# q and k padded from 40 to 48 rows per half in an mLSTM mixer kernel

## The chip, the cores and the metric

One Trainium2 chip, one core. The metric is the device time of one execution in microseconds (us), measured without the profiler; the profile is one more execution, taken by the hardware profiler.

## What is computed

Two layers over 4 batches of 768 tokens. The first is a gated linear attention (mLSTM) with 8 heads of 40 channels, the second a token mixer and a channel MLP.

```python
# per batch and head, for t in range(768):   (q, k, v: 40 channels)
C = f_stab * C + i_stab * outer(v[t], k[t])
n = f_stab * n + i_stab * k[t]
y[t] = sigmoid(o[t]) * (C @ q[t]) / max(abs(n @ q[t]), 1)
# x: the heads side by side, 768 x 320 per batch
u = x + (relu(x.T @ w_tok1) @ w_tok2).T
out = u + relu(u @ w_ch1) @ w_ch2
```

## The kernel before

The recurrence is done in chunks of 128 tokens: 6 chunks for each of 4 batches, 24 units (b, c). Inside a unit the scores of all 8 heads are a 128 x 128 matrix each: k times q over 40 channels (`st_s`, line 308, 16 instructions in PE's trace per 8 heads), which VectorE multiplies by a decay matrix (`st_p`, line 318); the product meets v on TensorE (`st_pv`, line 436). What comes from earlier chunks is a state C (`st_state`: line 374 reads it, line 382 updates it). The token mixer (`a_part`, `halves_b`) and the channel MLP (`gemm1`, `gemm1w`, `gemm2`) follow.

Batch 0 goes first, before there is anything else for TensorE to do; its six units run in the loop of lines 973 to 1032, each after the other, and the weights are decoded meanwhile: they come as 8-byte words by DMA (`dec_load`, line 650, tile `wst`) and pass ScalarE (lines 661 and 665), VectorE (line 679), ScalarE again (line 691) and GpSimd (line 697). From about 58 us on, the MLP of one batch and the attention of the next are interleaved on TensorE.

For the scores, q and k of a unit lie in HBM as `qk[b, c, hf]`: two halves of four heads, each 40 rows (channels) of 4,096 bytes (q and k, 4 heads, 128 tokens, f32). `load_qk` (line 220) brings half `hf` into partitions 64*hf to 64*hf+39 of the tile `raw`, of which there are three, used in turn by units 0, 1, 2, 3 and so on. The unused partitions 40 to 63 and 104 to 127 are never read: the matmul of line 308 takes `64 * hf:64 * hf + D`, D = 40.

Nearly every transfer is issued from SyncE's queue in the order of the program. In the start-up that order is: gates f (the gates i and the identity come from ScalarE's queue), qk of units 0 and 1 (four transfers), kv of unit 0, two `sig` (output gate), q3 of unit 1, qk of unit 2, kv of unit 1, q3, kv of unit 2, two `wst`, qk of units 3 and 4 (four transfers), two more `wst`, and so on. The loads of unit 3 stand at lines 948 and 949, those of unit 4 at 982 and 983. The scores take the two halves in turn, so they need both from their second head on:

```python
305        for h in range(4):
306            for hf in range(2):
307                r = t["raw"][64 * hf:64 * hf + D]
308                nc.tensor.matmul(t["s"][hf][:, h, :], r[:, 1, h, :], r[:, 0, h, :], start=True, stop=True)
```

ScalarE's order in the loop matters below too: for a unit c it first decodes two weight pieces (lines 661 and 665, twice), then makes `xh` (line 487), then `pq` (line 269) and `wcol` (line 145) of the unit after, which free a bank of the PSUM pool `ps_h` (two banks) for the next `spread_split` (lines 168, 183, 186).

Of the kernel before, what the change touches and what calls it, by code (L numbers as in the profile page):

```python
# [17 lines left out]
B, H, S, D = 4, 8, 768, 40  # L18
L = 128
NC = S // L  # L20
E1 = D + 1
DM = H * D
DT, DF = 256, 1536
NF = DF // 128
G3 = 3 * E1
HP = 9
# [9 lines left out]
def kernel(ctx: ExitStack, tc: tile.TileContext, gates, qk, q3, kv, og,  # L36
                            wt1, wt2, wc1, wc2, ident, out):
    nc = tc.nc
# [14 lines left out]
    def load_sig(b, i):  # L53
        t = ap.tile([128, NC // 2, DM], F32, tag="sig", name="sig", bufs=3)
        nc.sync.dma_start(out=t, in_=og[b].rearrange("(c p) e -> p c e", p=128)[:, 3 * i:3 * i + 3, :])
        sig[(b, i)] = t
# [47 lines left out]
    def state_mask():  # L104
        nc.gpsimd.memset(bm_t, 1.0)
        bm4 = bm_t.rearrange("p (g i e) -> p g i e", g=3, i=3)
        for s in (1, -1):
            nc.gpsimd.affine_select(bm4, bm4, pattern=[[0, 3], [-s * D, 3], [0, E1]], compare_op=ALU.is_ge,
                                    fill=0.0, base=0 if s > 0 else D - 1, channel_multiplier=s)
# [38 lines left out]
    def rows_w():  # L148
        w_row = sp.tile([128, DM + H * E1], F32, tag="kv", name="w_row")
        xpool[3] = w_row = w_row[0:B * HP, 0:(NC - 1) * L].rearrange("p (c t) -> p c t", t=L)  # L150
        p = phi.rearrange("p (c t) -> p c t", t=L)[:, 0:NC - 1, L - 1:L]
        nc.gpsimd.tensor_tensor(w_row, b_t[:, 0:(NC - 1) * L].rearrange("p (c t) -> p c t", t=L),
                                p.to_broadcast([B * HP, NC - 1, L]), ALU.add)
# [66 lines left out]
    def load_qk(u, hf):  # L220
        b, c = u
        t = T.setdefault(u, {})
        if hf == 0:
            t["raw"] = raws[units.index(u) % 3]
        nc.sync.dma_start(out=t["raw"][64 * hf:64 * hf + D], in_=qk[b, c, hf])

    def load_phi(u):
        b, c = u
# [7 lines left out]
    def load_kv(u):  # L236
        b, c = u
        if b == 0 and c == 2:
            kvt = sp.tile([128, DM + H * E1], F32, tag="kv", name="kvt")
        else:  # L240
            kvt = ap.tile([128, DM + H * E1], F32, tag="kv", name="kvt")
        nc.sync.dma_start(out=kvt, in_=kv[b, c * L:(c + 1) * L, :])
# [48 lines left out]
    def prep_kw(u):  # L291
        b, c = u
        if c == NC - 1:
            return
        t = T[u]
        kw = ap.tile([128, H * E1], F32, tag="kw", name="kw", bufs=2)
        kw = kw[:, 0:DM].rearrange("p (h d) -> p h d", d=D)
        nc.gpsimd.tensor_tensor(kw, t["kv"][:, 0:DM].rearrange("p (h d) -> p h d", d=D),
                                wcol[:, c, HP * b:HP * b + H].unsqueeze(2).to_broadcast([128, H, D]), ALU.mult)
# [228 lines left out]
    def att(b):  # L528
        for c in range(NC):
# [17 lines left out]
            if n2 and not ahead:  # L547
                load_qk(n2, 0)
                if joined(n1):
                    load_qk(n2, 1)  # L550
# [22 lines left out]
            if n2 and not ahead:  # L573
                if not joined(n1):
                    load_qk(n2, 1)
                if not th:
                    load_q3(n2)
# [345 lines left out]
    t = ps_m.tile([128, HP], F32, tag="m", name="gw")  # L923
# [254 lines left out]
def _layout(q, k, v, i_gate, f_gate, o_gate, moe_w_tok1, moe_w_tok2, moe_w_ch1, moe_w_ch2):  # L1178
    import numpy as np

    c = np.ascontiguousarray
    qt, kt = q.transpose(0, 1, 3, 2), k.transpose(0, 1, 3, 2)
    qk = np.stack([qt, kt], 1)[:, :, np.argsort(ROW)]
    qk = c(qk.reshape(B, 2, 2, 4, D, NC, L).transpose(0, 5, 2, 4, 1, 3, 6))
    q3 = np.zeros((B, 9, D, S), np.float32)
    q3[:, :H] = qt
    q3 = c(q3.reshape(B, 3, 120, NC, L).transpose(0, 3, 2, 1, 4))
    v1 = np.concatenate([v, np.ones((B, H, S, 1), np.float32)], 3)
    kv = c(np.concatenate([k.transpose(0, 2, 1, 3).reshape(B, S, DM),
                           v1.transpose(0, 2, 1, 3).reshape(B, S, H * E1)], 2))  # L1190
    og = c(o_gate.transpose(0, 2, 1, 3).reshape(B, S, DM))
    gates = np.zeros((2, B, HP, S), np.float32)
    gates[:, :, ROW] = np.stack([i_gate, f_gate])
    gates = gates.reshape(2, B * HP, S)

    bits = lambda a: c(a).view(np.int64)
    wt1 = bits(moe_w_tok1.reshape(NC, 128, DT).transpose(1, 0, 2).reshape(128, NC * DT))
    wt2 = bits(moe_w_tok2.reshape(2, 128, S).transpose(1, 0, 2).reshape(128, 2 * S))
    r3 = list(range(320)) + list(range(256, 320))
    wc1 = bits(moe_w_ch1[r3].reshape(3, 128, NF, 128).transpose(1, 2, 0, 3).reshape(128, NF * 384))  # L1200
    wc2 = bits(moe_w_ch2.reshape(NF, 128, DM).transpose(1, 0, 2).reshape(128, NF * DM))
    return dict(gates=gates, qk=qk, q3=q3, kv=kv, og=og, wt1=wt1, wt2=wt2, wc1=wc1, wc2=wc2,
                ident=np.eye(128, dtype=np.float32))
# [21 lines left out]
```

## Time and profile before

| | |
|---|---|
| Time, three executions without the profiler | 424.15, 423.2, 423.2 us (median 423.2) |
| The profiled execution's own time | 426.41 us |
| Its span, first to last instruction | 424.7 us |
| TensorE matmul busy | 98% of the span |
| VectorE, ScalarE, GpSimd busy | 65%, 43%, 33% |
| Mean granted TensorE clock | 0.996 of full |
| DMA | 52.34 MB |

The page gives the busy share of each engine in 40 slices of the span, with the granted TensorE clock and the DMA engines' share below; the chain of work that ended last; who waited for whom; and for a chosen stretch the sum of each engine's work. DMA share is the mean busy share of the core's 16 DMA engines, so 0.62 is ten of them.

### The profile page before, as it was taken

How to read it: one execution, taken by the hardware profiler on the slowest of the kernel's cores; microseconds unless marked ns; L12 is line 12 of the kernel's file. 1: busy time of each engine (PE TensorE's matmuls, PEld its weight loads, DVE VectorE, ACT ScalarE, POOL GpSimd, SP SyncE). 2: the span in 40 equal slices, each digit the busy share in tenths (PEclk: the TensorE clock that was granted, in tenths of full speed). 3: DMA queues.
4: the chain of work that ended last, by engine and by line, in shares of the span. 5: the costliest groups of instructions: out<-in, count | busy, mean ns of one | idle time of the engine just before them, and what ended most of it. 6: DMA issues, size and time to landing. Idle time of an engine off the chain costs nothing.

```text
span 424.7 us, 8974 instructions
## 1 busy us (share of the span) xinstructions
PE 417.6 (98%) x3504; PEld 396.4 (93%) x3504; DVE 277.9 (65%) x620; ACT 183.1 (43%) x429; POOL 139.7 (33%) x185
## 2 busy tenths in 40 slices
PE   8989999999999999999999999999999999999996
PEld 4879998889999999999999999999999999988996
DVE  7967665424867598799796698789786647111412
ACT  2768568794535546343334346234144112111111
POOL 7367678752544320340350230331441110000000
PEclk9989999999999999999999999999999999999999
DMA  7997758960785722443355031432420000000000
GB/s 204 261 271 235 252 180 292 293 177 15 242 238 186 213 69 78 150 117 102 111 162 184 31 109 31 145 119 89 125 86 32 0 22 12 0 0 2 33 30 31
DMA packets 24574, 52.34 MB, mean 123 GB/s; under 512 B 2565, under 2 KB 13325, under 8 KB 24533
## 3 DMA queue, kind: packets, MB, share of 16 engines
q1 hardware_dynamic: 24293, 51.61, 39.6%
q8 instruction: 27, 0.44, 0.4%
q10 hardware_dynamic: 240, 0.18, 0.1%
q14 instruction: 14, 0.11, 0.1%
HBM read 47.73 MB, written 4.04 MB: 122 GB/s over the span
## 4 chain that ended last, share of the span: by engine, by line
PE 95%; DMA 3%; DVE 1%; issue 0%; DVEq 0%
PE acc L703 30%; PE ps_h L824 21%; PE ps_h L850 11%; PE ps_sc L308 6%; PE ps_b L703 5%; PE ps_a L703 5%; PE po L436 5%; PE pu L382 3%; PE po L405 3%; DMA raw<-in_qk_dram 2%; PE po L374 2%; PE po L412 2%; PE ps_t L771 1%; PE ps_t L769 1%; PE ps_t L770 1%; DMA i_t<-in_gates_dram 1%
## 5 line engine op out<-in xcount | busy, mean ns | idle before, releaser
L824 PE MATMUL ps_h<-uT,c1h 128*128 128x256 f32 x480 | 91.4, 282 | 0.0
L703 PE MATMUL acc<-c2h,gh 128*128 128x320 f32 x288 | 89.0, 318 | 0.0
L836 ACT ACTIVATE gh<-ps_h 128x512 fp32r<-128x512 f32 x48 | 28.7, 598 | 135.5 <-PE ps_h L824 111.1
L703 PE MATMUL acc<-c2l,gh 128*128 128x320 f32 x288 | 86.4, 309 | 0.0
L824 PEld LDWEIGHTS ps_h<-uT,c1h 128*128 128x128 f32 x480 | 75.9, 188 | 0.5
L824 PE MATMUL ps_h<-uT,c1l 128*128 128x256 f32 x256 | 66.1, 281 | 0.0
L703 PE MATMUL acc<-c2h,gl 128*128 128x320 f32 x288 | 61.8, 309 | 0.0
L837 DVE SCALAR_TENSOR_TENSOR gl<-ps_h,gh 128x512 fp32r<-128x512 f32 x48 | 33.0, 687 | 40.0 <-ACT gh L836 39.5
L703 PEld LDWEIGHTS acc<-c2h,gh 128*128 128x128 f32 x288 | 54.1, 188 | 1.4
L703 PEld LDWEIGHTS acc<-c2l,gh 128*128 128x128 f32 x288 | 54.1, 188 | 0.9
L854 DVE SCALAR_TENSOR_TENSOR gl<-ps_h,gh 128x512 fp32r<-128x512 f32 x24 | 16.6, 691 | 49.1 <-ACT gh L853 49.1
L824 PEld LDWEIGHTS ps_h<-uT,c1l 128*128 128x128 f32 x256 | 48.1, 188 | 0.0
L703 PEld LDWEIGHTS acc<-c2h,gl 128*128 128x128 f32 x288 | 47.2, 188 | 0.0
L455 POOL TENSOR_TENSOR sig<-sig,ht 128x320 f32<-128x320 f32 x18 | 14.8, 822 | 97.7 <-DVE ht L416 89.8
L289 ACT ACTIVATE dd<-dd,bcol 128x128 f32<-128x128 f32 x144 | 45.8, 392 | 1.4 <-POOL dd L279 1.3
L850 PE MATMUL ps_h<-uT,c1h 128*128 128x512 f32 x120 | 36.0, 394 | 0.0
L318 DVE TENSOR_TENSOR dd<-ps_sc,dd 128x512 f32<-128x512 f32 x48 | 30.9, 682 | 6.9 <-PE ps_sc L308 6.8
L507 POOL TENSOR_TENSOR xl<-x,xh 128x320 fp32r<-128x320 f32 x18 | 15.8, 880 | 51.4 <-DVE xh L505 50.0
L853 ACT ACTIVATE gh<-ps_h 128x512 fp32r<-128x512 f32 x24 | 14.3, 595 | 41.2 <-PE ps_h L850 41.2
L308 PE MATMUL ps_sc<-raw 40*128 40x128 f32 x384 | 27.5, 281 | 1.9 <-DMA raw<-in_qk_dram 1.7
L308 PEld LDWEIGHTS ps_sc<-raw 40*128 40x128 f32 x384 | 23.7, 187 | 5.0 <-issue 2.1
L850 PEld LDWEIGHTS ps_h<-uT,c1h 128*128 128x128 f32 x120 | 22.1, 188 | 3.9
(151 smaller groups left out, 857.0 us busy)
## 6 DMA issues: line engine op xcount, KB each, us to landing
dd<-phi_d SPq DMA_DIRECT2D x18, 512.0 KB
wst<-in_wc_dram SPq DMA_DIRECT2D x22, 384.0 KB
kvt<-in_kv_dram SPq DMA_DIRECT2D x24, 324.0 KB
raw<-in_qk_dram SPq DMA_DIRECT2D x48, 160.0 KB
sig<-in_og_dram SPq DMA_DIRECT2D x8, 480.0 KB
out_dram<-x SPq DMA_DIRECT2D x24, 160.0 KB
q3t<-in_q_dram SPq DMA_DIRECT2D x20, 180.0 KB
wst<-in_wt_dram SPq DMA_DIRECT2D x8, 384.0 KB
```

Of the source, the lines that this page charges most:

```text
L289: nc.scalar.activation(dd[:, h, :], dd[:, h, :], AF.Exp, bias=bcol[:, c, HP * b + h:HP * b + h + 1])
L308: nc.tensor.matmul(t["s"][hf][:, h, :], r[:, 1, h, :], r[:, 0, h, :], start=True, stop=True)
L318: nc.vector.tensor_tensor(dd, t["s"][hf], dd, ALU.mult)
L436: nc.tensor.matmul(o, t["dd"][:, ROW[h], :], x, start=c == 0 and h == 0, stop=h == H - 1)
L455: nc.gpsimd.tensor_tensor(sg, sg, ht[:, :, 0:D], ALU.mult)
L507: nc.gpsimd.tensor_tensor(xl, x, f32(xh), ALU.subtract)
L703: nc.tensor.matmul(ps, a, m, start=(first and i == 0), stop=(last and i == n - 1))
L824: nc.tensor.matmul(ps[:, j, :], c1[x][:, a:a + 128], u[:, y, :], start=not opened and part is first and i == 0 and (order == 0 and not clo ...
L836: nc.scalar.activation(gh, ps, AF.Relu)
L837: nc.vector.scalar_tensor_tensor(gl, ps, 0.0, f32(gh), op0=ALU.max, op1=ALU.subtract)
L850: nc.tensor.matmul(ps, c1[x][:, a:a + 128], u[:, :, y, :], start=n == 0, stop=n == len(todo) - 1)
L854: nc.vector.scalar_tensor_tensor(gl, ps, 0.0, f32(gh), op0=ALU.max, op1=ALU.subtract)
```

## The change

The host lays q and k out with 48 rows per half, of which the last 8 are zeros, and `load_qk` brings all 48. Each transfer grows from 163,840 to 196,608 bytes. The matmuls read the same 40 rows as before; the number and the order of instructions on every engine are the same.

```diff
@@ -19,6 +19,7 @@
 E1 = D + 1
+DP = 48
 DM = H * D
@@ -222,7 +223,7 @@
         if hf == 0:
             t["raw"] = raws[units.index(u) % 3]
-        nc.sync.dma_start(out=t["raw"][64 * hf:64 * hf + D], in_=qk[b, c, hf])
+        nc.sync.dma_start(out=t["raw"][64 * hf:64 * hf + DP], in_=qk[b, c, hf])
@@ -1181,7 +1182,8 @@
     qk = np.stack([qt, kt], 1)[:, :, np.argsort(ROW)]
-    qk = c(qk.reshape(B, 2, 2, 4, D, NC, L).transpose(0, 5, 2, 4, 1, 3, 6))
+    qk = qk.reshape(B, 2, 2, 4, D, NC, L).transpose(0, 5, 2, 4, 1, 3, 6)
+    qk = c(np.concatenate([qk, np.zeros_like(qk[:, :, :, :DP - D])], 3))
```

## Rows read from the trace of the kernel before

**Rows 1.** The page, its head and sections 1 and 2.

```profile
span 424.7 us, 8974 instructions
PE 417.6 (98%) x3504; PEld 396.4 (93%) x3504; DVE 277.9 (65%) x620; ACT 183.1 (43%) x429; POOL 139.7 (33%) x185
...
PEclk9989999999999999999999999999999999999999
```

**Rows 2.** Who waited, TensorE alone, whole span: total us, times, longest.

```profile
PE ps_sc L308 <- DMA raw<-in_qk_dram: 1.7, 2, 1.0
PE warm L897 <- POOL zero L61: 1.4, 1, 1.4
PE ps_phi L183 <- DVE z L178: 0.4, 1, 0.4
```

**Rows 3.** Timeline of TensorE, 14 to 38 us: start, us, work, [idle before].

```profile
15.72 1.74 PE L308 MATMUL ps_sc<-raw 40*128 40x128 f32 x16
...
21.93 0.38 PE L186 MATMUL ps_phi<-id,z 128*128 128x512 bf16 x1
23.29 0.46 PE L308 MATMUL ps_sc<-raw 40*128 40x128 f32 x2 [0.98 <-DMA raw<-in_qk_dram]
24.44 1.13 PE L308 MATMUL ps_sc<-raw 40*128 40x128 f32 x14 [0.69 <-DMA raw<-in_qk_dram]
...
31.22 0.38 PE L168 MATMUL ps_phi<-late_b,id_b 128*128 128x512 bf16 x1
...
31.97 1.16 PE L308 MATMUL ps_sc<-raw 40*128 40x128 f32 x16
```

**Rows 4.** The chain of work that ended last, 0 to 60 us: start, us, what.

```profile
15.05 9.25 DMA raw<-in_qk_dram
...
25.91 1.35 PE po L374 x6
27.26 1.16 PE pu L382 x6
28.41 2.31 PE po L436 x16
...
33.48 0.79 PE po L374 x6
34.27 0.60 PE pu L382 x6
34.87 1.79 PE po L436 x16
```

**Rows 5.** Windows: length, busy by engine (PE, PEld, DVE, ACT, POOL), PEclk, DMA share, GB/s.

```profile
0.00:24.30 24.30, 20.84 (x172) 14.77 (x172) 19.93 (x41) 13.77 (x24) 14.54 (x32) 1.00 0.87 234
3.00:4.00 1.00, 1.00 (x4) 0.38 (x3) 0.69 (x2) 0.48 (x1) 0.91 (x2) 1.00 0.62 180
20.00:25.00 5.00, 3.33 (x33) 2.50 (x34) 3.16 (x12) 3.87 (x8) 4.58 (x7) 1.00 1.01 245
25.96:29.37 3.41, 3.41 (x18) 3.41 (x18) 1.47 (x4) 1.99 (x4) 0.73 (x1) 0.50 0.94 299
44.00:48.00 4.00, 4.00 (x34) 4.00 (x33) 2.63 (x10) 2.75 (x7) 3.83 (x6) 1.00 1.02 386
```

**Rows 6.** Timeline of SyncE's queue: DMA issues in the order of the program.

```profile
1.64 1.91 SPq L225 DMA_DIRECT2D raw<-in_qk_dram  x4
...
7.70 0.80 SPq L225 DMA_DIRECT2D raw<-in_qk_dram  x2
...
14.02 3.64 SPq L225 DMA_DIRECT2D raw<-in_qk_dram  x4
18.04 1.25 SPq L650 DMA_DIRECT2D wst<-in_wt_dram  x2
```

**Rows 7.** Timeline of ScalarE, 19 to 36 us.

```profile
28.46 0.52 ACT L661 ACTIVATE pf<-wst 128x384 f32<-128x384 f32 x1 [0.38 <-DMA wst<-in_wt_dram]
...
30.18 0.17 ACT L145 ACTIVATE wcol<-ps_q 128x9 f32<-128x9 f32 x1
```

**Rows 8.** Timeline of GpSimd, 16 to 25 us.

```profile
23.74 0.74 POOL L298 TENSOR_TENSOR kw<-kvt,wcol 128x320 f32<-128x320 f32 x1
```

## Prediction

> **What bounds the kernel now.** The page first: TensorE's matmuls are busy for 417.6 of 424.7 us [rows 1]. So a change to transfers can only pay where TensorE waits for one, or runs slowly because it waited. The list of its waits is short [rows 2]: 1.4 us at the very start, 0.4 us for VectorE, and 1.7 us in two waits for the transfer of q and k into `raw`. No wait of TensorE for any other transfer is in it, and none for `raw` after the start-up. The other 36 transfers of q and k, for batches 1 to 3, therefore cost nothing now.
>
> The timeline shows the two waits [rows 3]. The last matmul before ends at 22.31 (21.93 + 0.38). The scores of unit 3 begin at 23.29 after 0.98 us, do two matmuls and wait 0.69 us more for the other half, whose transfer was issued at 15.05 and took 9.25 us, to 24.30 [rows 4]. A third, smaller one hides in a busy row: the 16 score matmuls of unit 2, at 15.72, take 1.74 us, where the same 16 take 1.16 at 31.97 [rows 3], so 0.58 us are lost. Together 0.58 + 0.98 + 0.69 = 2.25 us.
>
> Then the clock. [...] What it costs is read from the chain, where the same work stands at both levels [rows 4]: 1.35 against 0.79, 1.16 against 0.60, 2.31 against 1.79 us, so 0.56 + 0.56 + 0.52 = 1.64 us. All that this change can give in the profiled execution is therefore 2.25 + 1.64 = 3.9 us.
>
> Why is the transfer late? From 20 to 25 us the 16 DMA engines are busy all the time (share 1.01) at 245 GB/s [rows 5]. The transfers are not short of issue, they stand in line: 9.25 us from issue to landing for 160 KB.
>
> **The change part by part.** *The engines.* From 3 to 4 us, when q and k of units 0 and 1 are nearly all that moves, the share is 0.62: ten of sixteen engines [rows 5]. 40 rows over ten engines are 4 packets of 4,096 bytes for each. I take it that 48 rows go over sixteen, 3 packets each. [...]
>
> *Price of a packet.* In the crowded window an engine moves 245 / (16 x 1.01) = 15.2 GB/s, so 4,096 bytes take 0.27 us; in the best window, 44 to 48 us, 386 / (16 x 1.02) = 23.7 GB/s and 0.17 us [rows 5]. Up to the transfer that lands at 24.30, eight of these transfers are issued: 4, 2, and the first 2 of the 4 from 14.02 on [rows 6]. The engines that carry them lose 8 packets each: 8 x 0.17 to 8 x 0.27 = **1.4 to 2.2 us earlier**, middle 1.8. The six others get 24 packets more, but they had none of these; all sixteen now carry the same.
>
> *Check by bytes, for a limit that all engines share.* By 24.3 us 234 GB/s x 24.3 us = 5.69 MB have moved [rows 5]. What stands in line up to that transfer, with the 8 padded ones, is 4.99 MB (gates 0.22, identity 0.07, q and k 1.57, three kv 1.00, two `sig` 0.98, two q3 0.37, two `wst` 0.79). The rest, 0.7 MB, are later transfers that the free engines have taken ahead. Even if the total rate stays 245 GB/s, the padded transfer lands 0.7 / 0.245 = 2.8 us earlier, because nothing runs ahead of it. Both ways of counting give a gain; I take 1.8, with 1.4 and 2.8 as ends.
>
> *At unit 2* six transfers are ahead: 6 x 0.17 = 1.0 us at least, more than the 0.58 us lost. That goes. *At unit 3* TensorE is then ready at 22.31 - 0.58 = 21.73, and the half lands at 24.30 - 1.8 = 22.5, so some 0.8 us of waiting stay and TensorE gains 1.8 us there. *The clock:* 0.8 us of idling instead of 1.67. The 0.58 us lost at 15.7 and the 0.4 us at 7.0 [rows 2, 3] were followed by no dip, so I take it that the slow stretch goes too: 1.8 + 1.64 = 3.4 us.
>
> *What is late next.* GpSimd's `kw` ends at 24.48 [rows 8]; TensorE would want it at 27.26 - 1.8 - 0.56 = 24.9 [rows 4]: just covered. ScalarE is tighter. The second L168 matmul, now at 31.22 [rows 3], needs the bank that L145 frees at 30.35, and that work stands behind two weight decodes, the later of which waits for its transfer until 28.46 [rows 7]. That transfer is the second `wst` after 18.04, with ten of the padded ones ahead of it [rows 6]: 10/8 x 1.8 = 2.25 us earlier (1.7 to 2.7 by packets). The bank is then free at 28.1, so TensorE cannot be more than 31.22 - 28.1 = 3.1 us ahead there (2.6 to 3.6). This is the smaller of 3.4 and 3.1: **the sum is 3.1 us.**
>
> *What costs nothing.* 1.57 MB more over 48 transfers: after 60 us the queue has slack and TensorE no wait for it [rows 2]. Instructions, their order and the matmuls are unchanged.
>
> The profiled execution took 426.41 us, so the sum makes it 423.3; the median of the runs without the profiler is 3.2 us lower, 423.2, and I take the same 3.1 us off it: **420.1 us**, 419.3 (all 3.9) to 420.6 (2.6) for this case.
>
> **The rivals.** *The slow clock stays.* 0.8 us of idling may still be followed by it; then TensorE gains only the 1.4 to 2.2 us of the landing: 421.4. For it: the row shows one dip and cannot tell which length of idling starts one.
>
> *The waits are the profiler's.* Profiled, the kernel takes 3.2 us longer than without, and waits plus slow clock come to 3.9 us. If recording slows the transfers, the plain runs may already have the half of unit 3 in time; then at most 0.7 us can be had: 423.0, no change. Against it: the transfers stand in line at a share of 1.0 over some 20 us, and such a line doesn't vanish by a small speed-up; the 3.2 us can also be a slower issue everywhere.
>
> *The rows' place is the limit, not the engines.* All 48 rows of a half go to partitions of one half of the tile, as the 40 did. If what bounds such a transfer is where it writes, sixteen engines share what ten had, and 20% more bytes take 20% longer. From 3 to 4 us these transfers ran at 180 GB/s [rows 5]: 163,840 bytes are 0.91 us, 196,608 are 1.09, so 0.18 us more each. The sixth makes unit 2 wait 1.1 us longer, the eighth lands 8 x 0.18 = 1.5 us later, at 25.8 instead of 24.30, and TensorE with it: 424.7, and more if the slow clock lasts longer. It decides as soon as that half lands after 24.30. [...]
>
> **How the numbers follow.** A measurement of this kernel can tell about 0.3%, 1.3 us, from no change. Forecast 0.50 and the clock that stays 0.13 are faster (0.02 more for gains in between): 0.65. The profiler's waits, 0.20, are no change. The ports, 0.15, are slower. The likeliest is 420.1. The range reaches from all 3.9 us gained (419.3, a little under for the byte count) over 421.4 and 423.0 to 423.9, and leaves out mainly the ports: 419.1 to 423.9.
>
> **What would show it.** Right: a DMA share near 1.0 from 3 to 5 us instead of 0.62; the half of unit 3 landing between 21.5 and 22.9; the 16 matmuls of unit 2 in about 1.16 us; no PEclk below full before the end; L145 of unit 3 ending near 28.1 with TensorE behind it by little. Wrong: a share of 0.62 or below (still ten engines), the half landing at 24.3 or later (the ports), or the waits gone from the profile and the time the same (the profiler).

## Result: slower by 1.2%

| | before | changed |
|---|---|---|
| median of 6 runs | 423.54 us | 428.64 us |
| lowest to highest | 423.2 to 424.15 | 426.44 to 431.72 |
| ratio, 95% interval | | 1.0121 (1.0079 to 1.0163) |
| profiled execution | 426.41 us, span 424.7 | 426.44 us, span 424.7 |

Ratios, here and below, are formed without runs that took over 1.5% more than the fastest of their kernel.

The two profiled executions took the same time, and that is a trap: the profiled one of before was slower than all six plain runs of that kernel, and the profiled one of the changed kernel was its fastest. So the two pages agree while the medians are 5.1 us apart. More profiles of both kernels were needed (experiments, below).

The page of the changed kernel, head and sections 1 and 2, against [rows 1]:

```profile
span 424.7 us, 8974 instructions
...
PE 417.0 (98%) x3504; PEld 396.0 (93%) x3504; DVE 280.0 (66%) x620; ACT 183.1 (43%) x429; POOL 138.6 (33%) x185
...
PEclk9989999999999999999999999999999999999999
```

Who waited, TensorE alone, changed kernel, against [rows 2]:

```profile
PE ps_sc L309 <- DMA raw<-in_qk_dram: 2.8, 2, 2.3
PE warm L898 <- POOL zero L62: 1.4, 1, 1.4
PE po L406 <- DVE p L346: 0.2, 1, 0.2
```

The wait for `raw` has not gone, it has grown from 1.7 to 2.8 us. Timeline of TensorE (start, us, work, [idle before]), against [rows 3]; all line numbers are one higher:

```profile
15.30 1.17 PE L309 MATMUL ps_sc<-raw 40*128 40x128 f32 x16
...
21.01 0.38 PE L187 MATMUL ps_phi<-id,z 128*128 128x512 bf16 x1
23.68 0.46 PE L309 MATMUL ps_sc<-raw 40*128 40x128 f32 x2 [2.29 <-DMA raw<-in_qk_dram]
24.62 1.13 PE L309 MATMUL ps_sc<-raw 40*128 40x128 f32 x14 [0.48 <-DMA raw<-in_qk_dram]
```

The 16 matmuls of unit 2 take 1.17 us instead of 1.74, as forecast, and TensorE comes to unit 3 at 21.39 (21.01 + 0.38) instead of 22.31. There it waits until nearly the same time as before (24.62 against 24.44 for the second half). The chain of waits (start, us, what), against [rows 4]:

```profile
14.46 10.02 DMA raw<-in_qk_dram
24.62 1.13 PE ps_sc L309 x14
...
26.09 1.22 PE po L375 x6
27.31 1.16 PE pu L383 x6
28.46 2.44 PE po L437 x16
...
33.66 0.79 PE po L375 x6
34.45 0.60 PE pu L383 x6
35.05 1.79 PE po L437 x16
```

The half of unit 3 lands at 24.48 (14.46 + 10.02) instead of the 22.5 that I forecast, and the stretch at half speed behind it is still there. Windows of the changed kernel (columns as in [rows 5]):

```profile
0.00:24.40 24.40, 20.46 (x172) 14.61 (x172) 19.46 (x41) 13.18 (x23) 14.93 (x32) 1.00 0.96 241
3.00:4.00 1.00, 1.00 (x4) 0.39 (x3) 0.86 (x3) 0.48 (x1) 0.90 (x2) 1.00 0.96 230
4.00:8.00 4.00, 4.00 (x27) 2.10 (x27) 3.77 (x8) 0.76 (x3) 3.61 (x7) 1.00 1.07 176
26.28:29.69 3.41, 3.41 (x19) 3.41 (x18) 2.14 (x6) 2.73 (x6) 1.08 (x2) 0.50 1.06 309
```

and two of the same windows before the change:

```profile
0.00:24.40 24.40, 20.84 (x172) 14.77 (x172) 20.01 (x42) 13.87 (x24) 14.64 (x32) 1.00 0.87 233
4.00:8.00 4.00, 3.56 (x21) 1.65 (x19) 3.69 (x8) 0.34 (x1) 3.59 (x8) 1.00 0.95 241
```

From 3 to 4 us the share is now 0.96 instead of 0.62 [rows 5]: sixteen engines do work. But from 4 to 8 us they are all busy and move 176 GB/s, where 241 were moved before. An engine needs 0.40 us for 4,096 bytes there (176 / (16 x 1.07) = 10.3 GB/s) instead of 0.26 (241 / (16 x 0.95) = 15.9 GB/s). Over the whole stretch to 24.4 us the rate is 8 GB/s higher, which is 0.20 MB; the zeros of the first eight transfers alone are 0.26 MB (8 x 8 rows x 4,096 bytes). So no more of the needed data has come by then, a little less.

### The profile page after: what moved, and what is told of

Its sections match the earlier page's. It is cut to its first block, busy times and chain, and to the rows that moved or that the text cites. A ratio compares the mean times of both kernels' runs of the same rounds, so it can differ in the third digit from the quotient of the medians.

```text
span 424.7 us, 8974 instructions
## 1 busy us (share of the span) xinstructions
PE 417.0 (98%) x3504; PEld 396.0 (93%) x3504; DVE 280.0 (66%) x620; ACT 183.1 (43%) x429; POOL 138.6 (33%) x185
## 4 chain that ended last, share of the span: by engine, by line
PE 92%; DVE 5%; DMA 2%; issue 0%; POOL 0%; ACT 0%; DVEq 0%; POOLq 0%
PE acc L704 29%; PE ps_h L825 19%; PE ps_h L851 11%; PE ps_sc L309 5%; PE ps_a L704 5%; PE ps_b L704 5%; PE po L437 5%; PE pu L383 3%; PE po L406 3%; DMA raw<-in_qk_dram 2%; PE po L413 2%; PE po L375 2%; PE warm L898 1%; DVE p L346 1%; DVE r L338 1%; DVE dd L319 1%
## 5 line engine op out<-in xcount | busy, mean ns | idle before, releaser
L309 PE MATMUL ps_sc<-raw 40*128 40x128 f32 x384 | 26.5, 280 | 2.8 <-DMA raw<-in_qk_dram 2.8
```

## Experiments

My theory after the result was the third rival: the place of the rows is the limit, six more engines only queue up at it, and whatever is behind them in their queues comes later. Its rivals: the 20% more bytes alone, or something in the later batches, and not the start-up.

**More profiles of the changed kernel, and one of before.** No edit; the same two kernels again (again48b, again48c and before_again are one profiled execution each).

> The changed kernel once more, for a second profile. [...] Theory B (the extra bytes in batches 1 to 3 disturb the weights and kv of the later stages): the start-up is as before and the time is lost after 60 us.

> The changed kernel, for one more profile, since its runs differ by up to 5 us. [...]

> As again48b, one more profile of the changed kernel: Theory 1, slow stretch near 24 to 30 us alone; Theory 2, a second one behind waits between 100 and 145 us.

> The kernel before once more, for a second profile: the one shown took 3.2 us more than the median of its other runs. [...]

Measured: again48 428.62 us over 4 runs, ratio 1.0112 (1.0063 to 1.016); again48b 429.73, again48c 432.56, before_again 422.96. In before_again TensorE has no wait for `raw` at all; this is the whole list of its waits:

```profile
PE warm L897 <- POOL zero L61: 1.4, 1, 1.4
PE ps_phi L168 <- ACT wcol L145: 0.8, 1, 0.8
```

Its half of unit 3 lands at 21.78 and its clock stays up to the end. So the waits of [rows 2] and the slow stretch of [rows 5] do not belong to a usual run of before; they belong to the one that was profiled. The mean granted clock on record for each run says the same: of 44 runs of before on two chips, 38 have 0.999 or 1.000 (421.95 to 425.03 us) and six of 0.988 to 0.996 (425.1 to 428.54 us); of the twelve runs of the changed kernel, eleven have 0.984 to 0.996. The changed kernel has the wait and the dip in each of its four profiles, and in the slowest two of them a second place, which before_again does not have. The chain of again48c there (start, us, what) and the two windows of low clock (columns as in [rows 5]):

```profile
118.87 10.63 DMA raw<-in_qk_dram
129.50 0.14 issue
129.64 1.13 PE ps_sc L309 x14
130.77 3.29 PE ps_h L825 x14
```

```profile
24.86:35.10 10.24, 10.24 (x55) 8.68 (x54) 6.13 (x18) 4.52 (x11) 4.58 (x6) 0.50 1.04 292
130.67:134.08 3.41, 3.41 (x17) 3.39 (x17) 1.23 (x3) 0.00 (x0) 1.96 (x2) 0.50 0.57 158
```

TensorE's waits of over 0.15 us past the first 20 us, and half of its time at a granted clock of 0.50 up to 150 us (an estimate; by [rows 4] and [rows 5] 1.64 of 3.41 us are lost), account for most of what sets these executions apart:

| profiled execution | us | waits | at clock 0.50 | lost | rest |
|---|---|---|---|---|---|
| before | 426.41 | 1.67 | 3.41 | 3.4 | 423.0 |
| before_again | 422.96 | 0.82 | 0 | 0.8 | 422.1 |
| changed | 426.44 | 2.77 | 3.41 | 4.5 | 422.0 |
| again48 | 428.24 | 3.68 | 3.4 | 5.4 | 422.9 |
| again48b | 429.73 | 2.96 | 6.8 | 6.4 | 423.4 |
| again48c | 432.56 | 3.21 | 13.65 | 10.0 | 422.5 |

The losses go from 0.8 to 10 us, the rest stays within 422.0 to 423.4. Among the four profiles of the changed kernel the waits are much alike, 2.8 to 3.7 us; what sets them apart is how long the clock stays low behind the waits, 3.4 to 13.65 us in all, half of which is counted as lost.

**Batch 0 alone, the later batches alone.**

```diff
-        nc.sync.dma_start(out=t["raw"][64 * hf:64 * hf + DP], in_=qk[b, c, hf])
+        n = DP if b == 0 else D
+        nc.sync.dma_start(out=t["raw"][64 * hf:64 * hf + n], in_=qk[b, c, hf, 0:n])
```

for start48 (and start48b, one profiled execution); `if b > 0` for late48 (and late48b).

> 48 rows for batch 0 alone (12 of the 48 transfers), 40 rows for batches 1 to 3. Theory A, loss in the start-up: as slow as the full change, about 428 us. Theory B, loss in the later stages: about 423.5 us, as before.

> 48 rows for batches 1 to 3 alone (36 transfers), 40 rows in the start-up. Theory A: about 423.5 us, as before. Theory B: about 428 us.

> 48 rows in batch 0 alone, for a second profile; its runs lay between 423.1 and 429.8 us. A run near 423: no wait over 0.6 us for q and k and no slow stretch. A run near 429: waits of 2 us or more for q and k of unit 3, and a slow stretch behind them.

> 48 rows in batches 1 to 3 alone, for a second profile; its runs lay between 423.4 and 426.7 us. Theory 2: a run near 426 has its waits between 100 and 145 us; the start-up is as in the kernel before.

Measured, ten runs each: start48 428.51 us (423.05 to 429.83), ratio 1.0061 (1.002 to 1.0101); late48 425.18 (423.37 to 426.72), ratio 1.0041 (1.0018 to 1.0063); start48b 428.42, late48b 424.45. By the ratios, with 423.49 us for before on that chip, the start-up costs 2.6 us (0.8 to 4.3) and the later batches 1.7 (0.8 to 2.7). The median of all ten runs of start48 is 5.0 us above before, but it lies in the upper of two groups: four runs at 423.05 to 425.57 and six at 428.35 to 429.83. Each group has a profile. The one of 423.05 waits 0.43 and 0.52 us at the two halves of unit 3 and has no dip before the end (the profile puts the second wait down to VectorE's `wf`, but the half lands at 23.08, just before its scores begin at 23.22):

```profile
22.24 0.46 PE L310 MATMUL ps_sc<-raw 40*128 40x128 f32 x2 [0.43 <-DMA raw<-in_qk_dram]
23.22 1.01 PE L310 MATMUL ps_sc<-raw 40*128 40x128 f32 x13 [0.52 <-DVE wf L681]
```

The one of 428.42 (start48b) waits 1.27 and 0.24 us there, less than the 2 us that I expected of such a run, and then comes this window:

```profile
24.71:34.95 10.24, 10.24 (x55) 8.68 (x54) 5.93 (x16) 4.56 (x11) 4.58 (x6) 0.50 1.04 290
```

Half of 10.24 is 5.1 us, and the waits differ by 0.56; together 5.7 us, where the two executions are 5.4 apart. The difference in the waits alone would hardly be measurable. In late48, where batch 0 has 40 rows, the start-up has no wait for `raw`; its unit 3 lands at 21.23, and the start-up wait that is left is for ScalarE's `wcol`. Timeline of TensorE in late48:

```profile
27.82 0.38 PE L169 MATMUL ps_phi<-late_b,id_b 128*128 128x512 bf16 x1 [0.50 <-ACT wcol L146]
```

and of ScalarE, whose work ends at 27.77:

```profile
27.61 0.16 ACT L146 ACTIVATE wcol<-ps_q 128x9 f32<-128x9 f32 x1
```

The later batches are not free either: late48 waits 0.78 us at 131.47 for VectorE's `dd`, late48b 0.94 us at 132.45. That is about half of the 1.7 us; where the rest goes was not found, and it is mostly not the clock, which is 0.998 or more in eight of the ten runs.

**The transfers alone.** Eight stretches of eight transfers of 4,096-byte rows, each stretch fenced off from the next by small VectorE copies:

```diff
+    def stretch(n, bases):
+        for i, t in enumerate(tiles):
+            p = bases[i % len(bases)]
+            nc.sync.dma_start(out=t[p:p + n], in_=rows[i * 128:i * 128 + n])
+        fence()
```

> Transfers alone, in eight stretches of eight with nothing beside them; the kernel computes nothing of the reference. All rows are 4,096 bytes. Stretches: 40 rows from partition 0; 48 from 0; 48 from 40; 32 from 0; 40 from 0 and from 64 in turn; 48 from 0 and from 64 in turn; 128 from 0; 16 from 0. Theory A (place): 48 rows from partition 0 run at about 200 GB/s, hardly more than 40 rows, in spite of sixteen engines, and the same 48 rows laid across both sides (from 40) run at 300 GB/s or more. If engines are the limit: 48 rows run at about 400 GB/s from either place, 40 rows at 250.

Measured: VectorE touches the eight tiles `ra` to `rh` in order and waits for each, so its timeline shows the spacing of the landings (start, us, work, [idle before]). The pieces are, in order: 40 rows from partition 0; 48 from 0; 48 from 40; 32 from 0; 40 from 0 and from 64 in turn; 48 the same; 128 rows; 16 rows.

```profile
11.23 0.16 DVE L51 TENSOR_TENSOR acc<-acc,rf 128x1 f32<-128x1 f32 x1 [1.10 <-DMA rf<-in_qk_dram]
12.49 0.16 DVE L51 TENSOR_TENSOR acc<-acc,rg 128x1 f32<-128x1 f32 x1 [1.10 <-DMA rg<-in_qk_dram]
...
18.80 0.16 DVE L51 TENSOR_TENSOR acc<-acc,rb 128x1 f32<-128x1 f32 x1 [0.99 <-DMA rb<-in_qk_dram]
...
25.06 0.16 DVE L51 TENSOR_TENSOR acc<-acc,rg 128x1 f32<-128x1 f32 x1 [1.07 <-DMA rg<-in_qk_dram]
...
31.04 0.16 DVE L51 TENSOR_TENSOR acc<-acc,rc 128x1 f32<-128x1 f32 x1 [1.32 <-DMA rc<-in_qk_dram]
...
33.72 0.16 DVE L51 TENSOR_TENSOR acc<-acc,rg 128x1 f32<-128x1 f32 x1 [0.60 <-DMA rg<-in_qk_dram]
...
37.59 0.16 DVE L51 TENSOR_TENSOR acc<-acc,rb 128x1 f32<-128x1 f32 x1 [0.53 <-DMA rb<-in_qk_dram]
...
40.81 0.16 DVE L51 TENSOR_TENSOR acc<-acc,rg 128x1 f32<-128x1 f32 x1 [0.48 <-DMA rg<-in_qk_dram]
...
45.81 0.16 DVE L51 TENSOR_TENSOR acc<-acc,rb 128x1 f32<-128x1 f32 x1 [0.75 <-DMA rb<-in_qk_dram]
...
50.15 0.16 DVE L51 TENSOR_TENSOR acc<-acc,rg 128x1 f32<-128x1 f32 x1 [0.56 <-DMA rg<-in_qk_dram]
...
56.37 0.16 DVE L51 TENSOR_TENSOR acc<-acc,rc 128x1 f32<-128x1 f32 x1 [1.23 <-DMA rc<-in_qk_dram]
...
60.71 0.16 DVE L51 TENSOR_TENSOR acc<-acc,rh 128x1 f32<-128x1 f32 x1 [0.65 <-DMA rh<-in_qk_dram]
...
69.51 0.16 DVE L51 TENSOR_TENSOR acc<-acc,rd 128x1 f32<-128x1 f32 x1 [1.13 <-DMA rd<-in_qk_dram]
...
73.33 0.16 DVE L51 TENSOR_TENSOR acc<-acc,rg 128x1 f32<-128x1 f32 x1 [1.12 <-DMA rg<-in_qk_dram]
...
77.45 0.16 DVE L51 TENSOR_TENSOR acc<-acc,ra 128x1 f32<-128x1 f32 x1 [1.95 <-DMA ra<-in_qk_dram]
...
80.62 0.16 DVE L51 TENSOR_TENSOR acc<-acc,rf 128x1 f32<-128x1 f32 x1 [0.48 <-DMA rf<-in_qk_dram]
```

Time per transfer, from the rows' differences: 40 rows from partition 0, 1.26 us; 48 from 0, (25.06 - 18.80) / 5 = 1.25; 48 from 40, (33.72 - 31.04) / 4 = 0.67; 32 from 0, 3.22 / 5 = 0.64; 40 in turn, 4.34 / 5 = 0.87; 48 in turn, 4.34 / 5 = 0.87; 128 rows, 3.82 / 3 = 1.27; 16 rows, 3.17 / 5 = 0.63. These are the steady parts of the stretches. In three of them (48 from 40, 48 in turn, 128) the third landing is held up once, by 0.5 to 1.0 us, for a reason that was not found, and is left out. With it, from the first issue to the last landing, the eight transfers in turn take 8.94 us with 40 rows and 9.37 with 48. So sixteen engines with three packets each were no faster here than ten with four, on one side or in turn on two (partitions 0 to 63 are one side here, 64 to 127 the other). A packet was not an engine's own price: in turn it is 0.87 / 4 = 0.22 us with ten engines and 0.87 / 3 = 0.29 with sixteen. And neither bytes nor engines set the time: 48 rows from 40 take little more than half of 48 rows from 0, 128 rows take as long as 48, and 16 as long as 32. Between 48 rows from 0 and 48 from 40, 1.25 and 0.67 us, only the place differs.

The six stretches whose transfers all go to the same place fall into two groups: 1.25 to 1.27 us for 40 or 48 rows from 0 and for 128 rows, 0.63 to 0.67 for 16 or 32 from 0 and for 48 from 40. What it is in the place that makes the two groups is not shown, and other row counts were not tried. The 0.87 in turn lies between: two transfers on different sides overlap (on one side they take 1.26 and 1.25), but not wholly; why not was not followed up.

What the changed kernel pays is therefore engine time. By these times, as an estimate, a unit (two halves) holds ten engines for 2 x 0.87 us before, 17.4 engine-us; sixteen for as long now, 27.8; as one transfer of 128 rows it would hold sixteen for 1.27, 20.3.

The kernels' own traces settle it, for they have every DMA packet with its size and time, and up to 25 us only q and k move in packets of 4,096 bytes. For the transfers of units 0 to 4 (the last two kernels are described below):

```
kernel          rows  packets  us per packet  engine-us per unit
before           40     400       0.237            19.0
before_again     40     400       0.216            17.3
late48           40     400       0.211            16.9
late48b          40     400       0.234            18.7
changed          48     480       0.323            31.0
again48          48     480       0.331            31.8
again48b         48     480       0.310            29.7
again48c         48     480       0.305            29.3
start48          48     480       0.290            27.8
start48b         48     480       0.298            28.6
split32        32 + 8   400       0.294            23.5
rows128          128    640       0.169            21.6
```

With 40 rows on ten engines a packet takes 0.21 to 0.24 us, with 48 on sixteen 0.29 to 0.33. On an engine that carries q and k, eight transfers are 32 packets of 0.224 on average, 7.2 us, before, and 24 of 0.310, 7.4 us, now. The ten engines gain nothing, and the other six, which had none, get 7.4 us of work each.

**Sixteen engines without more bytes**, the 40 rows as 32 and 8:

```diff
+        for r0, r1 in ((0, 32), (32, D)):
+            nc.sync.dma_start(out=t["raw"][64 * hf + r0:64 * hf + r1], in_=qk[b, c, hf, r0:r1])
```

> The kernel before with each half's 40 rows as two transfers, 32 rows and 8 rows: sixteen engines for four fifths of the rows and not one byte more. [...] If the change lost by its extra bytes alone and sixteen engines help: faster than before, 420 to 422 us.

Measured: 425.33 us, 423.9 to 432.03 over ten runs, ratio 1.0053 (1.0028 to 1.0078). No gain without the zeros either. It has twice as many transfers to issue, so its time doesn't isolate the bytes, and its profiled execution, its slowest, lost its time late (a 1.7 us wait for `dd` at 134 us and 13.65 us at a granted clock of 0.50 behind it). But the packets of its start-up do: without one byte more they take 0.294 us (table above), as long as with the zeros. So the extra bytes are not what makes a packet longer; sixteen engines on one side were enough here.

**One transfer of 128 rows per unit**, 64 rows per half, over both sides, for all batches (rows128) and for batch 0 alone (start128):

```diff
-DP = 48
+DP = 64
...
-        nc.sync.dma_start(out=t["raw"][64 * hf:64 * hf + DP], in_=qk[b, c, hf])
+        if hf == 0:
+            nc.sync.dma_start(out=t["raw"], in_=qk[b, c].rearrange("f d q h t -> (f d) q h t"))
```

> 64 rows per half (24 of zeros) and one transfer of 128 rows for a unit in place of two: 524,288 bytes instead of 2 x 196,608, over both sides. Place theory: transfers alone, 128 rows took 1.27 us and a pair of 48 rows about 1.76 us (a pair of 40 rows about 1.8), so a unit's q and k cost 0.5 us less in the queue in spite of a third more bytes; the scores of unit 3 have their data about 2 us earlier than with 40 rows; about 422 us, below the change by 1% or more and at or slightly below before. If bytes were what counts (2.6 times the zeros of the change): slower than the change, 430 us or more.

> The same for batch 0 alone; batches 1 to 3 load 40 rows twice as before. Place theory: about 422 us, like rows128 or a little below, since the later stages carry no extra bytes. If bytes count: between before and rows128.

Measured, ten runs each against 423.26 on that chip: rows128 **421.65 us** (421.03 to 422.32), ratio 0.996 (0.9941 to 0.9979); start128 421.71 (421.34 to 422.4), ratio 0.9968 (0.9956 to 0.998). This beats both kernels, before by 0.4%, with 60% more bytes of q and k than before and three times the zeros of the change, and within the noise all of it comes from batch 0. TensorE has no wait for `raw` in rows128; the whole list of its waits:

```profile
PE warm L899 <- POOL zero L62: 1.4, 1, 1.4
PE ps_phi L184 <- DVE z L179: 0.8, 1, 0.8
```

From 4 to 8 us its engines move 379 GB/s, where the changed kernel's moved 176 (windows, columns as in [rows 5]):

```profile
4.00:8.00 4.00, 3.23 (x26) 1.83 (x26) 3.77 (x8) 0.70 (x3) 3.60 (x8) 1.00 1.02 379
```

Unit 3 lands at 19.73. Its transfer is issued at 10.74, where the second half of unit 3 is issued at 14.19 in before_again and lands at 21.78, so the whole queue is ahead. How much of that is the transfer's shape and how much the halved number of issues on SyncE's queue was not separated.

**When each engine is done.** In the traces the semaphore of such a transfer steps sixteen times with 48 rows; with 40 rows it steps once at the issue and ten times later. That goes with the shares of 0.96 and 0.62 from 3 to 4 us, and a step is read here as one engine that is done. For the second half of unit 3, the first, the second to last and the last step (us; the one at the issue is left out):

```
kernel          engines  first  last but one  last
before             10    20.96     22.98     24.30
before_again       10    19.51     21.69     21.78
late48             10    19.52     21.01     21.23
late48b            10    20.18     21.22     21.89
changed            16    20.25     22.32     24.48
again48            16    20.47     22.04     24.98
again48b           16    20.73     22.96     24.35
again48c           16    20.53     22.47     24.00
start48            16    19.78     21.63     23.08
start48b           16    20.25     22.24     23.71
```

before_again, late48 and late48b have 40 rows in batch 0, in runs without a start-up wait of over 0.25 us for `raw`; their mean is 21.31 for the last but one and 21.63 for the last. The six with 48 rows have 22.28 and 24.10, 1.0 and 2.5 us later (with the profile of before among those of 40 rows, 0.6 and 1.8); 0.4 us of it stands already at the issue (14.53 against 14.08 on average). So the larger part is one engine: it lags behind the others by 1.4 to 2.9 us in every run with 48 rows, and by 1.3 us with 40 rows only in the unusual profile of before. It is not the number of engines alone: for unit 3 the lag is 0.8 us in rows128, and 0.04 in split32's transfer of 32 rows, both over sixteen engines.

In the transfers alone a lag stayed once it was there: in the three stretches that had a hold-up, the landings of a transfer's first and last engine lie 0.25 to 0.52 us apart before it and 0.93 to 1.54 in every transfer after it.

## Why the prediction was wrong

It said 420.1 us, faster; the third rival, **the rows' place is the limit**, with a chance of 0.15, happened. Step by step:

- *The engines*: right. Sixteen engines with 3 packets each were an assumption that no row of before shows; the changed kernel shows a share of 0.96 instead of 0.62 from 3 to 4 us, sixteen steps on the semaphore of a transfer, and 480 packets for ten transfers.
- *Price of a packet*: **this step failed.** It took 0.17 to 0.27 us as the price of a packet whatever else writes to the same side, so that three packets instead of four came out 1.4 to 2.2 us earlier over eight transfers. With ten engines the price was right, 0.21 to 0.24 us; with sixteen it rose to 0.29 to 0.33, so that eight transfers hold an engine 7.4 us instead of 7.2: the gain is nothing. Alone, in turn on both sides, it is the same, 0.87 us per transfer with four packets per engine and with three. The row that I had (180 GB/s from 3 to 4 us) could not separate the two readings, for ten engines at 0.17 to 0.27 us per packet give 150 to 240 GB/s too; I chose by the share of busy engines, and a full share said little of the rate here: 1.07 goes with 176 GB/s in the changed kernel, 1.02 with 379 in rows128.
- *"All sixteen now carry the same"*, taken as a gain: the same step's second half. The six engines without q and k had over 7 us for other transfers until unit 3; now they carry 24 packets of 0.31 us, 7.4 us, as well. The slowest of sixteen sets the landing: 23.08 to 24.98 us, against 21.23 to 21.89 in the usual runs with 40 rows, and 22.5 forecast. In place of 1.8 us earlier it is 2.5 us later, mean against mean. Why one engine lags, which is over half of it, is not shown; that the free time of the six engines hid such a lag before is argued, not shown.
- *Check by bytes*: it assumed that nothing runs ahead. By 24.48 us about 5.9 MB had moved (241 GB/s), 0.9 more than the 4.99 MB in line: other engines still ran ahead of the last one, as fifteen of them were done with unit 3 by 22.32.
- *Unit 2*: the number came, 1.17 us instead of 1.74 in the profiled execution, but by luck. Without the change the 16 matmuls take 1.16, 1.16 and 1.27 us (before_again, late48, late48b), with it also 1.56 and 1.43 (again48b, again48c).
- *The clock*: wrong with the landing. The 1.64 us in the sum are the same work at a granted clock of 0.50 and of 1.00 ([rows 4], [rows 5]), and that clock came back: the four profiles of the changed kernel have a dip behind the wait; it is 3.4 us long, as before, or 10.2, and the longer costs an estimated 5.1 us (half of it; start48b took 5.4 us more than start48's profile, with waits 0.56 longer). The first rival, the clock that stays, foresaw the dip, but with an earlier landing.
- *What is late next*: right in mechanism. Where `raw` comes in time, TensorE does wait for L145's bank: 0.82 us in before_again, 0.50 in late48. The bank is free at 27.8 to 28.3 there, near my 28.1, but without the padding of batch 0 by which I came to it.
- *What costs nothing*: wrong. The zeros of the later batches cost 1.7 us alone (late48), and in the slowest profile of the changed kernel a second `raw` is late, at about 129 us, 10.6 us after its issue.
- *The profiler's waits*, the second rival, was half right: not the recording, but this one execution was unusual. In before_again only 0.8 us of waiting was left, and the best layout tried, rows128, gained 1.6, so even a working change would have come to about 421.6 to 422.5, not 420.1. The 3.2 us between profile and median were the sign; I subtracted them and kept the whole gain of 3.1, which was thus mis-sized too.
- *The place, as priced*: right in sign, 424.7 against 428.64. The chances call this rival the ports; no run shows a port. What the runs show is a time that goes with where the rows lie: 48 rows take 1.25 us from partition 0 and 0.67 from 40. The half of unit 3 landed at 24.48, not 25.8, and unit 2 waited 1.1 us longer in none of the profiles. Its 0.18 us per transfer (20% more bytes at 180 GB/s) is not what happens (alone, 0.00 in the steady part and 0.05 over the whole stretch). Measured are more engine time, 28 to 32 engine-us per unit instead of 17 to 19, one engine that lags, and the slow clock behind the wait.

## What to carry to other kernels

Before giving a transfer more engines, time it alone, at the place where it writes, with the old and the new number of rows. Here 48 rows from partition 0 took as long as 40 (1.25 and 1.26 us), so the change only held more engines; one transfer of 128 rows over both sides brought a unit in packets of 0.17 us instead of 0.29 to 0.33, and the kernel to 421.65 us. The engines that a transfer does not use need not be idle in a crowded queue: with 40 rows on ten of them the share was 0.95 from 4 to 8 us and 1.01 from 20 to 25 [rows 5], so the other six had work. And when the profiled execution lies outside the plain runs, take a second profile before summing up its waits as what can be gained.

## What was not expected of the hardware

- The stretch at a granted clock of 0.50 behind a wait of TensorE came in two lengths in the start-up, 3.41 and 10.24 us, and 13.65 once later (split32). The waits of 0.98 and 0.69 us at unit 3 in before were followed by one, those of 0.43 and 0.52 in start48 were not. What decides the length stays open: waits of 2.29 and 0.48 us (changed) or 1.50 and 0.21 (again48b) were followed by 3.41 us, waits of 1.61 and 0.17 (again48c) or 1.27 and 0.24 (start48b) by 10.24.
- A packet of 4,096 bytes had no fixed price: alone, 0.22 us with ten engines and 0.29 with sixteen in the same arrangement, 0.39 where all sixteen write to one side (mean of the trace's packets), and 0.17 where 128 rows go over both.
- One engine lags. Every trace of these kernels has an instruction fetch of 16 KB, one packet of about 1.1 us, that starts between 14.5 and 17.5 us (16.8 us in the changed kernel, 17.3 in before, 16.3 in before_again), ahead of the late landing. But runs without a lag have it too (before_again; split32 at 15.6). Which engine it is on, and so whether it is the one that lags, is not shown; no run took the fetch away.
